# Attention with two expert layers: the gate's weight product moved behind attention, the output matrix decoded in PSUM, and edits at the start and before the experts

## The chip, the cores and the metric

The kernel runs on one core of one Trainium2 chip. The metric is the device time of one launch in microseconds. Every number of the trace comes from one profiled execution of the kernel before.

## The reference, cut to what matters

Causal attention over 4 batches of 8 heads (576 positions, head width 64) with a decay from a running sum of `s` feeds two layers. The first one multiplies by `w_in`, applies `h * clip(h + 3, 0, 6) / 6` and multiplies by `w_out`. The second one gives each of the 2304 tokens to one of 8 experts (288 tokens each), from the order of `x @ w_gate`, and runs that expert's two matrices.

```python
cum = np.cumsum(np.maximum(s, 0.0), axis=-1)
bias = -(cum[:, :, :, None] - cum[:, :, None, :])
scores = np.where(causal, -1e9, scale * (q @ k.T) + np.minimum(bias, 0.0))
attn_out = softmax(scores) @ v
...
h = x @ w_in
x2 = (h * np.clip(h + 3.0, 0.0, 6.0) / 6.0) @ w_out
...
logits = x2 @ w_gate
order = np.argsort(-logits.flatten())    # greedy, at most 288 tokens an expert
...
out[mask] = np.maximum(x2[mask] @ w1[e], 0.0) @ w2[e]
```

Logits have to be near exact, since they decide an order. So the kernel splits every f32 operand into two 16-bit parts (high and low) and sums three products.

## The kernel before, in words

**Attention** works on 16 pairs of heads. `prep` (L234) scales and splits q and k of a pair into `kq` and turns that tile with one DMA transpose on SP's queue (L253, 27 blocks of 128x128, tile `kqT`; slots 0 to 3 of it hold the first head, 4 to 7 the second, 8 the rest of both). It needs `CT`, the running sums in the layout of the positions, made once by `cumsums` (L196): PE transposes into one PSUM tile, then 18 copies on DVE (L216, L219). There is one `kq` buffer (KB=1), so the next pair is prepared only when the transpose has read it. `row_stage` finds row maxima (L298 on DVE), `col_stage` forms scores and exponentials (L364, L365 on ACT, L367 on POOL), `pv_stage` multiplies by v.

**The prologue** (`decode`, L495) reads `w_in` and then `w_out`, whose f64 words are turned into f32 by integer operations: ACT scales the high word (L511), DVE runs three operations (L512 to L514), ACT writes the f16 part (L516) and POOL the low part (L517). It does so for 32 tiles of 128x512, 16 of them for `w_out`. For `w_in` the intermediate tile lies in PSUM (tag "mm"), for `w_out` in SBUF (tag "g32", two buffers, shared with the activation of the first layer).

**The gate** (`gate_product`, L522). For eight deferred row tiles the logits are not computed from x2 but from the activation and `gm = w_out @ w_gate`, which has to be there before `logits(5)` (L580). For each of 16 slices of `w_out` two DMA transposes on SP's queue fill `wT` (one buffer), eight small matmuls on PE (L531, L532, 16 and 8 columns) go into the PSUM bank "tp", and DVE sums them into `gf` (L533).

**The first layer** (`mlp`, L634) goes through 9 units of 256 tokens: `h_step` (L548, matmuls at L556) and two `x2_tile`s (L591, L598 to L600) each. The row tiles of units 0 to 4 are done at once; for units 5 to 8 only `h_step` and `logits` run, and their eight tiles (10 to 17) are computed later, beside the routing, which is a chain of small operations on DVE and PE. Each x2 tile is stored to DRAM (`store_x2`, L624), from where the experts' tokens are gathered (L1111, POOL) and turned (L1119, SP).

**The last tile.** Expert 0's gather does not wait for tile 17: zeros are stored in its place at L853, and `tail(0)` (L1032) builds `lastsel`, a selection matrix; after the gather has been turned, four matmuls a half (L1211) pick tile 17's rows out of SBUF and DVE adds them to `xt` (L1213, two additions of 128x512).

**What sets the order.** The Python code writes the instructions in an order that `merge` (L62) makes: each stream is a generator that says how much PE time a step takes (or, by a negative number, how long it waits), and the stream with the smallest share of its budget goes next; `first=True` puts a stream ahead of the others whenever it is ready. The framework then assigns instructions to engines in the order of this program, by priority and by its own estimate of when each is ready; every engine runs its list strictly in order. In attention, each of 18 stages merges its three parts with the prologue, the gate and the first layer (15.5 us of PE time a stage). After the last stage `att_stack` is closed and the pool `late` takes its memory; then the rest of the first layer is written out alone.

```python
gts.budget = GB if t >= GT0 else 0.0
ml.budget = FILL
merge(streams + [x for x in (pro, gts, ml) if x.alive])
...
GT["keys"] = ready_keys
ml.budget = None
merge([ml])
```

Of the kernel before, what the change touches and what calls it, by code (L numbers as in the profile page):

```python
# [34 lines left out]
GB = 1200.0  # L35
# [8 lines left out]
GT0 = 2  # L44
# [57 lines left out]
def tile_attention_moe(ctx, tc, q, k, v, s, w_in, w_out, w_gate, w1, w2, out):  # L102
# [93 lines left out]
    def cumsums():  # L196
# [17 lines left out]
        for r in range(3):  # L214
            for t in range(NB):
                nc.vector.tensor_copy(CT[:, :, t:8:4, r],  # L216
                                      p[:, r, t, :].rearrange("p (n h) -> p n h", h=2))
            for h in range(2):
                nc.vector.tensor_copy(CT[h * 64:(h + 1) * 64, :, 8, r],  # L219
                                      p[h * 64:(h + 1) * 64, r, 4, h:B * H:2])  # L220
# [13 lines left out]
    def prep(n):  # L234
# [18 lines left out]
        pin(nc.sync.dma_start_transpose(out=t.rearrange("p s w x -> p (s w) x"), in_=kq.rearrange("p s w x -> p (s w x)")))  # L253
# [208 lines left out]
    def wsl(w, f):  # L462
        return w[f // 8][:, (f % 8) * 512:(f % 8 + 1) * 512]
# [31 lines left out]
    def decode(i):  # L495
        raw = RAW.pop(i)
        for f in range(2):
# [6 lines left out]
            if i < FP:  # L504
                y = psum.tile([128, 512], F32, name="mm", tag="mm", bufs=2)
            else:
                y = wts.tile([128, 512], F32, name="down", tag="g32", bufs=2)
            m = wts.tile([128, 512], F32, name="mag", tag="r", bufs=2)
            m3, y3 = (x.rearrange("p (c x) -> p c x", c=KC) for x in (m, y))
            a3 = y3.bitcast(I32) if i < FP else m3.bitcast(I32)  # L510
# [11 lines left out]
    def gate_product(fs):  # L522
        for f in fs:
            o = wts.tile([128, 2, KC, 128], F16, name="wT", bufs=1)
            o = (o[:, 0], o[:, 1].bitcast(BF))
            for t, w in zip(o, (woh, wol)):
                nc.sync.dma_start_transpose(out=t, in_=wsl(w, f))
            yield -DL[2]
            p = psum.tile([128, 16], F32, name="tp", tag="tp", bufs=TPB)
            for c in range(KC):  # L530
                nc.tensor.matmul(p, o[0][:, c, :], wgh[:, c, :], start=(c == 0), stop=False)  # L531
                nc.tensor.matmul(p[:, 0:8], o[1][:, c, :], wgh[:, c, 0:8], start=False, stop=(c == KC - 1))  # L532
            nc.vector.tensor_reduce(gf[:, f], p.rearrange("p (a e) -> p e a", a=2), axis=AX.X, op=OP.add)  # L533
            yield 8 * 27.0
# [56 lines left out]
    def x2_tile(t):  # L591
# [15 lines left out]
        if t == NT - 1:  # L607
            GT["last"] = xo
        else:
            store_x2(t, xo)  # L610
# [109 lines left out]
    gts = Stream(gates(), FT1 * 660.0)  # L720
# [30 lines left out]
    for t in range(NST):  # L751
# [16 lines left out]
    while pro.alive or gts.alive:  # L768
        raws()
        pro.budget = gts.budget = 4000.0  # L770
        merge([x for x in (pro, gts) if x.alive])
    att_stack.close()
    cpsum = ctx.enter_context(tc.tile_pool(name="cpsum", bufs=1, space=bass.MemoryType.PSUM))
    late = ctx.enter_context(tc.tile_pool(name="late", bufs=1))
    g_stack = ExitStack()
# [77 lines left out]
    store_x2(NT - 1, none)  # L853
# [37 lines left out]
    merge([ml])  # L891
# [140 lines left out]
    def tail(ph, r):  # L1032
# [19 lines left out]
        if ph == 0:  # L1052
            for j, x in ((1, RW - 128 % RW), (2, 0)):
                w = RW - x
                o = 0 if j == 1 else 128 - RW
                nc.vector.tensor_tensor(lastsel[:, o:o + w], ohr[:, NT - 1, x:],
                                        e3[:, NT - 1, j:j + 1].to_broadcast([128, w]), op=OP.mult)
# [203 lines left out]
```

## Time and profile before

| | us |
|---|---|
| median of 3 runs | 935.71 |
| lowest and highest run | 931.65, 938.3 |
| the profiled execution's own time | 931.17 |
| its span, first to last instruction | 929.4 |
| PE busy in the span | 834.4 (90%) |
| DVE, POOL, ACT busy | 568.3, 472.6, 374.9 |
| mean granted TensorE clock | 0.949 of full speed |

A share of the whole span is an average over stages: attention alone, attention with the first layer (to about 460 us), deferred units, deferred tiles with the routing (to about 684 us), and the experts. The rows below are therefore taken stage by stage. A DMA's issue is shown on SP's queue; when it lands is seen from who waits for it.

### The profile page before, as it was taken

The page shows a single profiled execution, that of the slowest core. Times are in us where ns is not written, and L with a number is a line of the kernel's source. Part 1 is how long each engine was busy: PE and PEld are TensorE (multiplying, and loading weights), DVE is VectorE, ACT ScalarE, POOL GpSimd, SP SyncE. Part 2 cuts the span into 40 slices and gives each one's busy share as a digit, 9 for nine tenths or more (in the row PEclk, how much of TensorE's full clock was granted, in tenths as well). Part 3 has the DMA queues.
Part 4 walks back from the last instruction along what each step waited for, and adds up shares of the span by engine and source line. Part 5 has one row for each costly group of instructions (what it writes and reads, how often), then busy time and mean ns, then how long its engine had stood idle before and what let it go on. Part 6 is the DMA issues. An engine that isn't in the chain of part 4 may idle for free. (4 is left out here: it accounts for less than half of the span.)

```text
span 929.4 us, 21469 instructions
## 1 busy us (share of the span) xinstructions
PE 834.4 (90%) x8553; PEld 595.1 (64%) x8553; DVE 568.3 (61%) x1705; ACT 374.9 (40%) x704; POOL 472.6 (51%) x485
## 2 busy tenths in 40 slices
PE   1688678777899999999999999999979999999996
PEld 0356457544565875866958988444447777778885
DVE  7988889875555564541356455675757877772221
ACT  2576655544344554544202222002214554455641
POOL 1466656655253564563433333003346787788951
PEclk9986778989789999999999999999989999999998
DMA  7888888789844645323220000032355765777820
GB/s 181 193 207 208 187 176 231 155 156 199 169 86 102 129 90 104 63 41 63 28 52 7 2 1 1 13 128 100 104 157 152 209 186 162 207 242 203 207 68 26
DMA packets 225524, 116.04 MB, mean 125 GB/s; under 512 B 202224, under 2 KB 202224, under 8 KB 225424
## 3 DMA queue, kind: packets, MB, share of 16 engines
q1 hardware_dynamic: 222352, 105.24, 48.1%
q0 software_dynamic: 3072, 9.44, 3.3%
q8 instruction: 67, 1.10, 0.5%
q14 instruction: 33, 0.27, 0.1%
HBM read 69.30 MB, written 9.70 MB: 85 GB/s over the span
## 5 line engine op out<-in xcount | busy, mean ns | idle before, releaser
L556 PE MATMUL mm<-xT,W 128*128 128x256 f16 (+3 forms) x2304 | 209.7, 251 | 6.1 <-DVE g L564 6.1
L1106 POOL TENSOR_TENSOR W<-stg,W 128x512 bf16<-128x512 f32 x128 | 145.0, 1159 | 100.7 <-ACT W L1104 99.8
L556 PEld LDWEIGHTS <-W 128*128 128x128 f16 (+1 forms) x2304 | 177.9, 99 | 22.9 <-DVE g L564 4.0
L1128 PEld LDWEIGHTS <-W 128*128 128x128 f16 (+1 forms) x1536 | 145.5, 98 | 42.5 <-issue 6.4
L367 POOL TENSOR_TENSOR eh<-e,eh 128x512 f16<-128x512 f32 (+1 forms) x100 | 105.5, 1070 | 99.5 <-ACT eh L365 96.6
L577 POOL TENSOR_TENSOR g<-g,g 128x512 f16<-128x512 f32 x72 | 85.5, 1187 | 125.7 <-DVE g L576 112.9
L284 PE MATMUL sc<-kqT 96*128 96x64 f16 (+10 forms) x480 | 104.7, 303 | 32.8 <-DMA kqT<-kq 18.2
L599 PE MATMUL mm<-W,g 128*128 128x512 bf16 x288 | 110.2, 383 | 3.3 <-POOL W L517 3.2
L600 PE MATMUL mm<-W,g 128*128 128x512 f16 x288 | 110.4, 384 | 0.0
L598 PE MATMUL mm<-W,g 128*128 128x512 f16 x288 | 109.6, 383 | 0.7 <-DVE g L564 0.7
L1128 PE MATMUL mm<-xt,W 128*128 128x288 f16 x768 | 105.1, 290 | 5.4 <-DVE xt L1213 4.6
L1128 PE MATMUL mm<-ht,W 128*128 128x288 f16 x768 | 102.6, 286 | 0.0
L562 ACT ACTIVATE r<-mm,three 128x512 f32<-128x512 f32 x72 | 49.4, 686 | 124.3 <-PE mm L556 116.5
L284 PEld LDWEIGHTS <-kqT 96*128 96x128 f16 (+5 forms) x768 | 54.5, 110 | 67.7 <-issue 27.2
L298 DVE TENSOR_REDUCE mx<-sc 128x1 f32<-128x384 f32 (+2 forms) x144 | 69.6, 511 | 38.0 <-PE sc L295 20.5
L364 ACT ACTIVATE e<-sc 128x512 f32<-128x512 f32 (+1 forms) x112 | 59.4, 538 | 70.0 <-PE sc L352 58.1
L564 DVE SCALAR_TENSOR_TENSOR g<-r,mm 128x512 f32<-128x512 f32 x72 | 49.3, 685 | 53.4 <-ACT r L562 52.8
L419 PE MATMUL pv<-v,eh 128*128 128x65 f16 (+1 forms) x480 | 71.4, 209 | 6.0 <-DVE x L432 6.0
L1104 ACT ACTIVATE W<-stg 128x512 f16<-128x512 f32 x128 | 75.4, 621 | 0.0
L421 PE MATMUL pv<-v,eh 128*128 128x65 f16 (+1 forms) x480 | 70.6, 205 | 1.8 <-POOL eh L367 1.8
L420 PE MATMUL pv<-v,eh 128*128 128x64 f16 (+1 forms) x480 | 71.0, 207 | 0.0
L365 ACT ACTIVATE eh<-e 128x512 f16<-128x512 f32 (+1 forms) x112 | 60.9, 570 | 13.9 <-PE pv L421 11.6
(225 smaller groups left out, 1370.3 us busy)
## 6 DMA issues: line engine op xcount, KB each, us to landing
stg<-in_moe_w_dram SPq DMA_DIRECT2D x32, 1024.0 KB
raw<-in_moe_w_in_dram SPq DMA_DIRECT2D x8, 1024.0 KB
raw<-in_moe_w_out_dram SPq DMA_DIRECT2D x8, 1024.0 KB
x2d<-xo SPq DMA_DIRECT2D x18, 256.0 KB
ldq<-in_q_dram SPq DMA_DIRECT2D x32, 128.0 KB
ldk<-in_k_dram SPq DMA_DIRECT2D x32, 128.0 KB
ldv<-in_v_dram SPq DMA_DIRECT2D x32, 128.0 KB
ldq<-in_q_dram SPq DMA_DIRECT2D x16, 32.0 KB
```

The source lines that it names most:

```text
L284: nc.tensor.matmul(o, x[0:kq], y[0:kq], start=start, stop=stop)
L367: eng.tensor_tensor(t[:, 1], e, t[:, 0], op=OP.subtract)
L419: nc.tensor.matmul(oj[:, 0:65], e[0], vv[:, 0:65], start=a, stop=False)
L420: nc.tensor.matmul(oj[:, 0:64], e[0], vv[:, 66:130], start=False, stop=False)
L556: nc.tensor.matmul(p[:, f, at:at + w], wsl(wt, ft)[:, c * 128:(c + 1) * 128], XT[b][:, c, hl, i:i + w], start=(n == 0), stop=(n == 3 * KC ...
L577: nc.gpsimd.tensor_tensor(g[:, 1].rearrange("p f x -> p (f x)"), g32, g[:, 0].rearrange("p f x -> p (f x)"), op=OP.subtract)
L598: nc.tensor.matmul(p, g[:, 0], wsl(woh, f), start=(f == 0), stop=False)
L599: nc.tensor.matmul(p, g[:, 0], wsl(wol, f), start=False, stop=False)
L600: nc.tensor.matmul(p, g[:, 1], wsl(woh, f), start=False, stop=(f == FT1 - 1))
L1104: nc.scalar.activation(h, x, AF.Copy)
L1106: nc.gpsimd.tensor_tensor(l, x, h, op=OP.subtract)
L1128: nc.tensor.matmul(p, wt[:, c, o * 128:(o + 1) * 128], x(hl, c), start=(n == 0), stop=(n == last))
```

## The change

It moves the gate's stream out of attention: its transposes go to three buffers of the pool `late`, two slices ahead of the products, and it is merged, with first right, with the rest of the first layer. It gives the decoding of `w_out` the PSUM bank "tp" (one buffer) for its intermediate tile. `cumsums` copies in four instructions. Pair 0's transpose is issued in two parts, slots 0 to 3 by SP and 4 to 8 by ACT. And the two last tiles (16 and 17) instead of one are kept out of expert 0's gather: two stores of zeros, two selection matrices, six additions instead of two. The expert outputs get three buffers of one tag.

```diff
@@ cumsums
-        for r in range(3):
-            for t in range(NB):
-                nc.vector.tensor_copy(CT[:, :, t:8:4, r],
-                                      p[:, r, t, :].rearrange("p (n h) -> p n h", h=2))
-            for h in range(2):
-                nc.vector.tensor_copy(CT[h * 64:(h + 1) * 64, :, 8, r],
-                                      p[h * 64:(h + 1) * 64, r, 4, h:B * H:2])
+        for h in range(2):
+            nc.vector.tensor_copy(CT[:, :, 4 * h:4 * h + 4, :],
+                                  p[:, :, 0:4, h:B * H:2].rearrange("p r t n -> p n t r"))
+            nc.vector.tensor_copy(CT[h * 64:(h + 1) * 64, :, 8, :],
+                                  p[h * 64:(h + 1) * 64, :, 4, h:B * H:2].rearrange("p r n -> p n r"))
@@ prep
-        pin(nc.sync.dma_start_transpose(out=t.rearrange("p s w x -> p (s w) x"), in_=kq.rearrange("p s w x -> p (s w x)")))
+        for eng, s0, s1 in ((nc.sync, 0, 9),) if n else ((nc.sync, 0, 4), (nc.scalar, 4, 9)):
+            pin(eng.dma_start_transpose(out=t[:, s0:s1].rearrange("p s w x -> p (s w) x"),
+                                        in_=kq[:, s0:s1].rearrange("p s w x -> p (s w x)")))
@@ decode
-            if i < FP:
-                y = psum.tile([128, 512], F32, name="mm", tag="mm", bufs=2)
-            else:
-                y = wts.tile([128, 512], F32, name="down", tag="g32", bufs=2)
+            y = psum.tile([128, 512], F32, name="down", tag="mm" if i < FP else "tp", bufs=2 if i < FP else TPB)
...
-            a3 = y3.bitcast(I32) if i < FP else m3.bitcast(I32)
+            a3 = y3.bitcast(I32)
@@ the gate
-    def gate_product(fs):
-        for f in fs:
-            o = wts.tile([128, 2, KC, 128], F16, name="wT", bufs=1)
...
+    def gate_turn(f):
+        o = GT["late"].tile([128, 2, KC, 128], F16, name="wT", tag="xg", bufs=3)
+        o = (o[:, 0], o[:, 1].bitcast(BF))
+        for t, w in zip(o, (woh, wol)):
+            nc.sync.dma_start_transpose(out=t, in_=wsl(w, f))
+        return o
...
     def gates():
-        for i in range(FP, 2 * FP):
-            yield from wait(lambda: ST["w"] > i)
-            yield -DL[1]
-            yield from gate_product((2 * (i - FP), 2 * (i - FP) + 1))
+        turned = []
+        for f in range(FT1 + 2):
+            if f < FT1:
+                turned.append(gate_turn(f))
+            if f >= 2:
+                gate_product(f - 2, turned[f - 2])
+                yield 8 * 27.0
+            yield -2500.0
...
-    gts = Stream(gates(), FT1 * 660.0)
+    gts = Stream(gates(), FT1 * 216.0, first=True)
...
-        gts.budget = GB if t >= GT0 else 0.0
         ml.budget = FILL
-        merge(streams + [x for x in (pro, gts, ml) if x.alive])
+        merge(streams + [x for x in (pro, ml) if x.alive])
...
-    merge([ml])
+    merge([gts, ml])
@@ the last tiles
-    store_x2(NT - 1, none)
+    for t in range(NT - 2, NT):
+        store_x2(t, none)
...
-            for j, x in ((1, RW - 128 % RW), (2, 0)):
...
+            for k, sel in enumerate(lastsel):
+                o = 0
+                for j in range(3):
+                    x = max(0, CAP - 128 * (k + 1) - j * RW)
...
-            yo = (wts, wts, ffn)[j].tile([RW, DM], F32, name="yo", tag=("wT", "x2T", "yo")[j], bufs=1)
+            yo = ffn.tile([RW, DM], F32, name="yo", bufs=3)
...
-    store_x2(NT - 1, GT["last"])
-    sp = tokens(0, sp)
+    with tc.high_priority(offset=HP):
+        sp = tokens(0, sp)
...
-    for hl in range(2):
-        p = mm_tile([128, KC, 128])
...
+    for k in (1, 0):
+        last, w = GT["last", k], 128 * (k + 1)
+        store_x2(NT - 1 - k, last)
+        with tc.high_priority(offset=HP):
+            for c0 in range(0, 2 * KC, 512 // w):
+                cs = range(c0, c0 + 512 // w)
+                p = cpsum.tile([128, len(cs), w], F32, name="pick", tag="y", bufs=YB)
...
+                x = xt[:, cs.start:cs.stop, CAP - w:]
+                nc.vector.tensor_tensor(x, x, p, op=OP.add)
```

## Rows read from the trace of the kernel before

**Rows 1.** Windows: us; PE, PEld, DVE, ACT, POOL busy (x); PEclk, DMA share, GB/s.
```profile
140.00:200.00 60.00, 48.84 (x504) 36.21 (x502) 54.67 (x90) 32.78 (x57) 39.70 (x33) 0.95 0.79 181
...
200.00:262.00 62.00, 47.05 (x443) 29.48 (x440) 31.04 (x75) 23.91 (x44) 23.49 (x23) 0.83 0.88 177
...
262.00:460.00 198.00, 197.69 (x2499) 145.73 (x2498) 94.77 (x218) 91.49 (x162) 101.72 (x93) 0.99 0.40 77
...
460.00:510.00 50.00, 48.67 (x432) 34.60 (x430) 27.58 (x134) 7.38 (x11) 18.10 (x58) 0.98 0.21 34
...
684.00:691.00 7.00, 1.81 (x12) 1.07 (x13) 2.89 (x12) 0.19 (x1) 0.59 (x1) 0.82 0.54 123
```

**Rows 2.** PE's waits from 140 to 200 us: total us, times, longest us.
```profile
PE tp L531 <- DMA wT<-W: 5.2, 4, 2.1
...
PE mm L556 <- DVE g L564: 4.1, 3, 2.2
```

**Rows 3.** PE's waits from 200 to 262 us, same columns.
```profile
PE tp L531 <- DMA wT<-W: 8.9, 4, 4.1
...
PE mm L599 <- POOL W L517: 2.2, 3, 1.0
```

**Rows 4.** Timeline of the start: start us, us, engine, line, operation, count, idle before.
```profile
10.22 0.71 DVE L216 COPY CT<-tp 128x32 f16<-128x32 f16 x4
...
12.67 0.62 DVE L219 COPY CT<-tp 64x16 f16<-64x16 f16 x2
...
13.86 4.17 SPq L253 DMA_TRANSPOSE kqT<-kq  x1
...
19.94 0.50 PE L284 MATMUL sc<-kqT 99*128 99x384 f16 x1 [11.41 <-DMA kqT<-kq]
```

**Rows 5.** Timeline of PE: first and 25th of a run of gate-sized matmuls.
```profile
503.73 0.17 PE L585 MATMUL mm<-gm,g 128*128 128x16 f16 x1
...
504.34 0.17 PE L585 MATMUL mm<-gm,g 128*128 128x16 f16 x1
```

**Rows 6.** Timeline of one pair of wT transposes, and its second product's start.
```profile
187.66 2.52 SPq L527 DMA_TRANSPOSE wT<-W  x2
...
191.41 0.18 PE L532 MATMUL tp<-wgh,wT 128*128 128x8 f16 x1
```

**Rows 7.** Groups on DVE, 135 to 242 us: count, busy us, mean ns, idle before.
```profile
L513 DVE SCALAR_TENSOR_TENSOR mag<-raw,mag 128x512 int32<-128x512 int32 x16 | 17.8, 1117 | 0.2
L514 DVE SCALAR_TENSOR_TENSOR mag<-raw,mag 128x512 int32<-128x512 int32 x16 | 13.2, 827 | 0.0
L512 DVE TENSOR_SCALAR mag<-down 128x512 int32<-128x512 int32 x16 | 8.6, 540 | 9.6 <-ACT down L511 9.6
```

**Rows 8.** Instructions of the same lines with PSUM operands: ns min/median/max, first and last start.
```profile
L512 DVE TENSOR_SCALAR mm<-mm x16: 680/690/699, 14.1 to 115.2; 128x512 int32<-128x512 int32 x16
...
L513 DVE SCALAR_TENSOR_TENSOR mm<-raw,mm x16: 678/689/708, 15.3 to 116.4; 128x512 int32<-128x512 int32 x16
...
L514 DVE SCALAR_TENSOR_TENSOR mag<-raw,mm x16: 666/678/689, 16.5 to 119.5; 128x512 int32<-128x512 int32 x16
```

**Rows 9.** Groups on DVE, 140 to 262 us: the reductions of the gate's products.
```profile
L533 DVE TENSOR_REDUCE gf<-tp 128x8 f32<-128x16 f32 x16 | 2.7, 167 | 8.2 <-PE tp L532 8.1
```

**Rows 10.** Timeline after attention: first use of the late pool, the store of zeros.
```profile
465.23 0.14 POOL L787 IOTA prio<- 128x8 f32 x1 [2.82 <-issue]
...
469.33 0.32 SPq L625 DMA_DIRECT2D x2d<-none  x1
```

**Rows 11.** Timeline before the experts: index, store of tile 16, gather, first add.
```profile
672.08 0.15 DVE L1068 SCALAR_TENSOR_TENSOR idx<-ids,ic 96x3 int32<-96x3 f32 x1
...
672.85 0.34 SPq L625 DMA_DIRECT2D x2d<-xo  x1
...
675.96 1.14 POOL L1111 DMA_INDIRECT xg<-x2d,idx  x1 [0.25 <-DVE rb L936]
...
688.90 0.69 DVE L1213 TENSOR_TENSOR xt<-xt,mm 128x512 f16<-128x512 f16 x1 [3.89 <-DMA xt<-xg]
```

More of the change, by code (lines that the diff above doesn't have):

```diff
@@ L34 @@
 WAFT = 1
-GB = 1200.0
 LG = 14
@@ L43 @@
 HE = 2
-GT0 = 2
 RD = 0
@@ L520, in tile_attention_moe, with gate_product @@
     gf = wts.tile([128, FT1, 8], F32, name="gf")
-    def gate_product(fs):
-        for f in fs:
-            o = wts.tile([128, 2, KC, 128], F16, name="wT", bufs=1)
[L525 to L534, printed above, removed]
+    def gate_turn(f):
[4 more added lines that the diff above has]
+        return o
+    def gate_product(f, o):
+        p = psum.tile([128, 16], F32, name="tp", tag="tp", bufs=TPB)
+        for c in range(KC):
+            nc.tensor.matmul(p, o[0][:, c, :], wgh[:, c, :], start=(c == 0), stop=False)
+            nc.tensor.matmul(p[:, 0:8], o[1][:, c, :], wgh[:, c, 0:8], start=False, stop=(c == KC - 1))
+        nc.vector.tensor_reduce(gf[:, f], p.rearrange("p (a e) -> p e a", a=2), axis=AX.X, op=OP.add)
     ST = {"x": 0, "w": 0, "g": 0, "rx": 0, "gx": 0}
@@ L606, in x2_tile @@
         nc.vector.tensor_tensor(xo[:, 1], p, xo[:, 0], op=OP.subtract)
-        if t == NT - 1:
-            GT["last"] = xo
+        if t >= NT - 2:
+            GT["last", NT - 1 - t] = xo
         else:
@@ L763, in tile_attention_moe @@
         pro.budget = PB[min(t, len(PB) - 1)] * 1000.0
-        gts.budget = GB if t >= GT0 else 0.0
         ml.budget = FILL
-        merge(streams + [x for x in (pro, gts, ml) if x.alive])
+        merge(streams + [x for x in (pro, ml) if x.alive])
     flush()
-    while pro.alive or gts.alive:
+    while pro.alive:
         raws()
-        pro.budget = gts.budget = 4000.0
-        merge([x for x in (pro, gts) if x.alive])
+        pro.budget = 4000.0
+        merge([pro])
     att_stack.close()
@@ L774, in tile_attention_moe @@
     late = ctx.enter_context(tc.tile_pool(name="late", bufs=1))
+    GT["late"] = late
     g_stack = ExitStack()
@@ L1052, in tail @@
         if ph == 0:
-            for j, x in ((1, RW - 128 % RW), (2, 0)):
[L1054 to L1057, printed above, removed]
+            for k, sel in enumerate(lastsel):
+                o = 0
+                for j in range(3):
+                    x = max(0, CAP - 128 * (k + 1) - j * RW)
+                    w = RW - x
+                    if w > 0:
+                        nc.vector.tensor_tensor(sel[:, o:o + w], ohr[:, NT - 1 - k, x:],
+                                                e3[:, NT - 1 - k, j:j + 1].to_broadcast([128, w]), op=OP.mult)
+                        o += w
         rhs = rt([128, NT, 2, 3], "rhs", F16)
@@ L1069, in tail @@
         IDX[ph] = idx
-    lastsel = late.tile([128, 128], F16, name="lastsel")
+    lastsel = [late.tile([128, 128 * (k + 1)], F16, name=f"lastsel{k}") for k in range(2)]
     SCAT = []
@@ L1204, in tile_attention_moe @@
     ffn = ctx.enter_context(tc.tile_pool(name="ffn", bufs=1))
-    store_x2(NT - 1, GT["last"])
-    sp = tokens(0, sp)
+    with tc.high_priority(offset=HP):
+        sp = tokens(0, sp)
     xt = XTS[0]
-    for hl in range(2):
-        p = mm_tile([128, KC, 128])
-        for c in range(KC):
-            nc.tensor.matmul(p[:, c], GT["last"][:, hl, c * 128:(c + 1) * 128], lastsel, start=True, stop=True)
-        x = xt[:, KC * hl:KC * (hl + 1), CAP - 128:]
-        nc.vector.tensor_tensor(x, x, p, op=OP.add)
+    for k in (1, 0):
[5 more added lines that the diff above has]
+                p = cpsum.tile([128, len(cs), w], F32, name="pick", tag="y", bufs=YB)
+                for c in cs:
+                    nc.tensor.matmul(p[:, c - c0], last[:, c // KC, c % KC * 128:(c % KC + 1) * 128], lastsel[k],
+                                     start=True, stop=True)
+                x = xt[:, cs.start:cs.stop, CAP - w:]
+                nc.vector.tensor_tensor(x, x, p, op=OP.add)
     for ph in range(E8):
```

## The prediction

> **What bounds the kernel now.** I read the windows first, because the share of the whole span mixes stages. From 262 to 460 us PE is busy 197.69 of 198 us, at a granted clock of 0.99: there only less work on PE helps [rows 1]. Before that it is otherwise. From 140 to 200 us PE is busy 48.84 of 60 and DVE 54.67 of 60, so DVE is nearly full. From 200 to 262 us PE is busy 47.05 of 62, DVE only 31.04, ACT and POOL less, and the granted clock is down to 0.83 of full speed [rows 1]. Nothing is full there, so somebody waits. Then I read PE's waits in these two stretches. The largest is the gate's first matmul, which waits for `wT`: 5.2 us before 200 us and 8.9 us after it, together 14.1 of the 26.1 us in which PE is idle (60 less 48.84 and 62 less 47.05) [rows 1 to 3]. Next come DVE's activation (4.1 us) and the decoded output matrix from POOL (2.2 us) [rows 2, 3]. So an order of work in which PE stands before a transposed weight slice costs more than half of PE's idle time of this stage, and `gm`, which it makes, is not used before 503.73 us, where its first reader starts [rows 5].
>
> **The start: four copies and two queues.** The 18 copies to `CT` run from 10.22 to 13.29 us (12.67 plus 0.62), 3.07 us, and the transpose of pair 0 is issued at 13.86 us, just behind them [rows 4]. The trace has no copy of the new shapes (192 and 48 elements). Below, each costs no less than one old copy's share of the row, 0.71/4 = 0.18 us, so four take 0.7; above, no more than a PSUM operation of 512 columns, 0.69 us [rows 8], so 2.8. I take 1.2, near the small ones. That gains 1.9 us, between 0.3 and 2.4. PE has nothing to do then: its first score matmul waits 11.41 us for this transpose [rows 4].
>
> The transpose takes 4.17 us to issue for 27 blocks, 0.154 us a block, and is there at 19.94 us, 1.9 us after its last issue [rows 4]. Split into 12 blocks on SP and 15 on ACT, and both at once, the longer half takes 2.3 us: a gain of 1.9 us. One behind the other, each with its landing, it is 1.85 + 1.9 + 2.3 + 1.9 = 7.95 us instead of 6.08: a loss of 1.9 us, softened by the first head's part coming earlier. No row shows transposes of two queues in flight, so I take the middle, 0. ACT's issue stands ahead of ACT's first decoding and its preparation of pair 1; pair 1 waits for this transpose anyway, since there is one `kq` buffer. The Trainium skill speaks against the two queues: "DMA: Bandwidth & Descriptors", section "Silent corruption: two transposing streams in flight at once", says that the later stream's first transpose must wait until all of the earlier stream's have completed. By that rule the halves run one behind the other, and the forecast would be 1.9 us longer; no row here shows it.
>
> **The gate leaves attention.** PE loses 128 matmuls. Their pitch shows where the same shapes run without waits: 24 steps from 503.73 to 504.34 us, 0.0254 us each [rows 5], so 3.3 us in all (their busy time is longer, since it overlaps). With the waits of 14.1 us this is 17.4 us of PE time at most. SP's queue loses 32 transposes, 16 pairs of 2.52 us [rows 6], 40 us in which the loads and the transposes of later pairs stood behind them. DVE loses 16 reductions, 2.7 us [rows 9].
>
> **The decoding in PSUM.** Per tile of 128x512 DVE's three operations take 540 + 1117 + 827 = 2484 ns in SBUF [rows 7] and 690 + 689 + 678 = 2057 ns with PSUM operands [rows 8]: 0.43 us less, 6.8 us for 16 tiles. Against it stands the one bank: ACT's scaling of the next tile has to wait until DVE's third operation on this one is done, so two tiles of a load no longer overlap. Behind that instruction on ACT stand exponentials of `col_stage`, for which POOL and then PE wait. ACT has room (busy 32.78 of 60 and 23.91 of 62 [rows 1]), but the decoding of the last loads is a chain, load after load, and I allow up to 5 us of loss for it.
>
> **What of this shortens the stage.** From 140 to 200 us DVE is the limit, so PE's waits there are worth only what DVE is relieved of: about 9 of 16 tiles and reductions, 9/16 x (6.8 + 2.7) = 5 us. From 200 to 262 us DVE has room. PE can win 8.9 us of waits and half of the matmuls, 1.7 us; what is late next is the decoded matrix (2.2 us so far) [rows 3], so I take three quarters, 8 us. With fewer gaps the granted clock of 0.83 may come back to the 0.95 of the stretch before it [rows 1]: 47.05 x (1 - 0.83/0.95) = 6 us at most, of which I take 4. Sum: a gain of 17 us. The ends are 17.4 + 6 + 2 for DVE = 25 us of gain, and 5 us of loss if nothing is won and the one bank delays the last loads.
>
> **The gate behind attention.** There PE is nearly full (48.67 of 50 us from 460 to 510 us [rows 1]), so the 3.3 us of matmuls are paid. The transposes can't start before the pool `late` has its memory, which its first user shows at 465.23 us, and perhaps only behind the zeros, stored at 469.33 us [rows 10]. A pair and the arrival of its second part took 191.41 - 187.66 = 3.75 us [rows 6], so the first product has its data between 469 and 473 us. By the program it stands some 6 us behind the end of attention's matmuls. With three buffers later slices are requested some 8 us ahead, more than these 3.75, so I see a wait at the first products only: 3 us, between 0 and 8. The stores and transposes of tiles 8 and 9 stand on SP behind at most a pair, 2.5 us, which nothing waits for soon. The chain ends at 465.23 to 469.33 plus 16 x 2.52 plus 2, 507 to 512 us, so `logits(5)`, now at 503.73, is 4 to 8 us late; unit 6's matmuls can cover that, if they stand ahead of it on PE. Cost: 6.3 us, between 3.3 and 19.
>
> **The last two tiles.** Expert 0's index is ready at 672.23 us, but the gather starts at 675.96, 3.1 us behind the store of tile 16 at 672.85 [rows 11]. That wait goes: up to 3.7 us, less the longer `lastsel`, three more small operations on the same chain, of 0.15 us like the index's own. But behind the transposes DVE now makes six additions of 0.69 us [rows 11], and the first expert matmul needs the fifth instead of the first: 4 x 0.69 = 2.8 us more. So PE's idle time before the experts (5.2 of 7 us from 684 to 691 us [rows 1]) stays about as it is: 0, between 3.1 us of gain and 2.8 of loss. The expert outputs' buffers I cost at nothing, since their number stays three; if one came late it would show as a wait of ACT for a scatter.
>
> **Sum.** -1.9 + 0 - 17 + 6.3 + 0 = -12.6 us against the profiled execution's 931.17 us, of which 929.4 is span: 918.6 us. That execution lies 4.5 us below the median of the three runs, 935.71, so the median to be expected is about 923 us.
>
> **The rivals.**
> *Everything is won.* The two queues overlap, all waits of the gate go, the clock comes back, the first products find their data: -2.4 - 1.9 - 25 + 3.3 - 3.1 = -29 us, 907. For it speaks that the waits are PE's largest; against it the full DVE before 200 us. Chance 0.15.
> *The stage keeps its length.* DVE before 200 us, and behind it the chain of loads through one bank, take the place of the gate's waits, and only 3 us are won: -1.9 - 3 + 6.3 = +1.4 us, 937. For it speaks DVE's 54.67 of 60 us; against it that DVE is half idle after 200 us. Chance 0.2.
> *The gate stalls the full engine (slower).* In attention its products cost PE 14.1 us of waits although they had a whole stage's slack in the program. If they are placed behind attention as much too early again, the same 14.1 us fall on an engine that has no gaps, with up to 8 us before `logits(5)`: 3.3 + 14.1 + 8 = 25 us, and -1.9 - 17 + 25 = +6; where the gain in attention is only half, +15. That is 942 to 951, say 946. It decides from a cost of 19 us behind attention, where it eats the gain. For it speaks that the order is estimated and not measured; against it the three buffers and an SP queue with little else. Chance 0.13.
> The forecast keeps 0.52.
>
> **How the numbers follow.** The forecast's own range is 916 to 931. The range reaches from 908, beside the first rival, to 940, which takes in the second; outside lie most of the third and some of the first. A measurement of this kernel can tell about 1% from no change, here 926.4 and 945.1 us. Faster by more: 0.15 and three quarters of the forecast, 0.54. Slower by more: most of the third rival and a tail, 0.13. Within 1%: 0.33.
>
> **What would show it.** Right, if between 140 us and the end of attention no wait for `wT` is left, the first use of the pool `late` (465.23 us [rows 10]) comes some 19 us earlier, DVE's three decoding operations take near 0.69 us each, and the first scores start 0 to 4 us earlier. Wrong in the third term, if PE's idle time in these stretches is only renamed, to DVE's activation or to the decoded matrix. Wrong in the fourth, if PE waits behind attention for `wT` by more than some 4 us, or stands before `logits(5)`. The fifth shows in PE's gap before the first expert matmul, now 5.2 us. The forecast as a whole fails if attention ends less than 8 us earlier.

## The result and the profile after

The kernel after takes 926.14 us (median of 5 runs, 923.98 to 927.23) against 935.71 in the same comparison: ratio 0.9911, interval 0.9887 to 0.9934. The forecast was 923. A second comparison on another chip gave 922.41 against 928.74, ratio 0.9934 [0.9911, 0.9957]. The kernel before measured 927 to 936 us from chip to chip, so below only ratios and positions inside a trace are compared. The profiled execution took 926.86 us with a span of 924.7, which is 4.7 less than before (before's profiled execution lies 4.5 us below its median, after's 0.7 above); where those went is read from three marks, which cut the span into three parts that add up. `late` is the first use of the pool `late` (the end of attention), the second mark is the first store of a deferred tile (the end of the stage that pays for the gate).

| | before | after | difference |
|---|---|---|---|
| start to `late` | 465.23 | 448.46 | -16.8 |
| `late` to the first deferred store | 130.4 | 144.6 | +14.3 |
| from there to the end | 333.8 | 331.6 | -2.2 |

The windows of the kernel after, core 0, with the columns of [rows 1]:

```profile
140.00:200.00 60.00, 51.31 (x505) 37.47 (x504) 52.67 (x97) 37.12 (x69) 40.90 (x36) 0.94 0.75 183
200.00:262.00 62.00, 53.04 (x528) 35.66 (x527) 39.35 (x81) 30.75 (x57) 31.67 (x32) 0.92 0.77 156
460.00:510.00 50.00, 43.29 (x494) 34.09 (x493) 21.43 (x101) 6.95 (x11) 9.24 (x8) 0.93 0.50 88
684.00:691.00 7.00, 6.29 (x54) 4.69 (x54) 6.45 (x29) 3.52 (x8) 2.90 (x4) 1.00 0.28 89
```

Against [rows 1], PE is 2.5 us busier from 140 to 200 us and 6 us busier from 200 to 262, where the granted clock is 0.92 instead of 0.83. From 460 to 510 us it has 6.7 us of idle time where there was 1.3. Now PE's waits, from 200 to 262 us and, under the dots, from 440 to 510:

```profile
PE mm L594 <- POOL W L512: 5.4, 5, 1.8
PE tp L615 <- DMA x2T<-xo: 1.4, 1, 1.4
...
PE tp L528 <- DMA wT<-W: 5.5, 6, 1.5
PE mm L580 <- DVE gm L690: 1.6, 1, 1.6
PE tp L527 <- issue: 1.2, 1, 1.2
PE tp L527 <- DMA wT<-W: 1.1, 1, 1.1
```

The waits for `wT` have left attention, and PE's idle time from 140 to 262 us falls from 26.1 to 17.7 us. That is less than the waits for `wT` had been, since a part of them only got another name: what is late next there is the decoded matrix from POOL, 5.4 us where it was 2.2 [rows 3]. The waits for `wT` stand behind attention instead. SP's queue shows why (a line is a run of issues of one kind):

```profile
448.44 3.81 SPq L521 DMA_TRANSPOSE wT<-W  x3
452.48 0.86 SPq L620 DMA_DIRECT2D x2d<-none  x2
453.39 11.70 SPq L521 DMA_TRANSPOSE wT<-W  x9
465.14 0.58 SPq L620 DMA_DIRECT2D x2d<-xo  x1
465.76 1.30 SPq L608 DMA_TRANSPOSE x2T<-xo  x1
467.17 11.30 SPq L521 DMA_TRANSPOSE wT<-W  x8
478.51 0.58 SPq L620 DMA_DIRECT2D x2d<-xo  x1
479.14 1.29 SPq L608 DMA_TRANSPOSE x2T<-xo  x1
480.54 17.85 SPq L521 DMA_TRANSPOSE wT<-W  x12
```

From 448.44 to 498.39 us the queue issues 32 transposes, 1.27 to 1.49 us apart in the mean of a run, with stores and `x2T` between. It has few pauses; its own waits in that time (446 to 500 us) are mostly for PE to free one of the three buffers, 5.2 us:

```profile
SPq L521 <- PE mm L551: 2.3, 1, 2.3
SPq L521 <- PE mm L595: 1.9, 2, 1.1
SPq L521 <- PE tp L528: 1.0, 1, 1.0
```

The work that PE has ahead of `logits(5)` was 503.73 - 465.23 = 38.5 us long before [rows 5, 10], and with the gate's matmuls 41.8. SP needs more, about 45 us even without its waits. So the first matmul of `logits(5)` starts 53.3 us behind `late`, which is 14.8 us more than before: the whole loss of the stage lies ahead of it.

```profile
501.79 0.17 PE L580 MATMUL mm<-gm,g 128*128 128x16 f16 x1 [1.61 <-DVE gm L690]
```

The decoding (groups by line, DVE, 140 to 440 us) costs what was forecast, 690 ns an operation:

```profile
L508 DVE SCALAR_TENSOR_TENSOR down<-raw,down 128x512 int32<-128x512 int32 x15 | 10.3, 689 | 0.2
L509 DVE SCALAR_TENSOR_TENSOR mag<-raw,down 128x512 int32<-128x512 int32 x15 | 10.2, 681 | 0.4
L507 DVE TENSOR_SCALAR down<-down 128x512 int32<-128x512 int32 x14 | 9.7, 692 | 3.0 <-ACT down L506 3.0
```

The start (timeline of ACT, SP and PE, with SP's wait between) and the first expert matmul (PE), to be held against [rows 4] and [rows 11]:

```profile
11.80 1.42 ACTq L250 DMA_TRANSPOSE kqT<-kq  x1
SPq L250 <- DMA kqT<-kq: 6.3, 1, 6.3
16.20 1.56 SPq L250 DMA_TRANSPOSE kqT<-kq  x1
20.04 0.50 PE L282 MATMUL sc<-kqT 99*128 99x384 f16 x1 [11.51 <-DMA kqT<-kq]
685.22 0.41 PE L1132 MATMUL mm<-xt,W 128*128 128x288 f16 x2 [0.19 <-DVE xt L1223]
```

The copies end at 11.21 instead of 13.29 us and the transpose starts 2.1 us earlier, but its second half is issued only 4.4 us behind the first, since SP's queue waits until the first half has landed (6.3 us, the line in the middle), and the first scores come at 20.04 us, as before (19.94).

### The profile page after: what moved, and what is told of

The parts are those of the page before. It is cut to its first block, busy times and chain, and to the rows that moved or that the text cites. A ratio compares the mean times of both kernels' runs of the same rounds, so it can differ in the third digit from the quotient of the medians.

```text
span 924.7 us, 21475 instructions
## 1 busy us (share of the span) xinstructions
PE 824.6 (89%) x8561; PEld 588.6 (64%) x8561; DVE 554.3 (60%) x1698; ACT 373.3 (40%) x704; POOL 467.4 (51%) x485
## 5 line engine op out<-in xcount | busy, mean ns | idle before, releaser
L551 PE MATMUL mm<-xT,W 128*128 128x256 f16 (+3 forms) x2304 | 205.3, 248 | 5.4 <-DVE g L559 3.8
L282 PE MATMUL sc<-kqT 96*128 96x64 f16 (+10 forms) x480 | 102.1, 295 | 40.3 <-DMA kqT<-kq 22.4
L1132 PE MATMUL mm<-xt,W 128*128 128x288 f16 x768 | 103.0, 286 | 2.6 <-DVE ht L1146 2.2
L282 PEld LDWEIGHTS <-kqT 101*128 101x128 f16 (+5 forms) x768 | 52.9, 107 | 72.2 <-DMA kqT<-kq 26.4
L417 PE MATMUL pv<-v,eh 128*128 128x65 f16 (+1 forms) x480 | 67.7, 203 | 1.9 <-DVE x L430 1.9
L419 PE MATMUL pv<-v,eh 128*128 128x65 f16 (+1 forms) x480 | 66.5, 199 | 2.0 <-POOL eh L365 2.0
L418 PE MATMUL pv<-v,eh 128*128 128x64 f16 (+1 forms) x480 | 66.9, 201 | 1.0 <-DVE v L220 1.0
```

Source lines behind the costliest of these rows:

```text
L282: nc.tensor.matmul(o, x[0:kq], y[0:kq], start=start, stop=stop)
L417: nc.tensor.matmul(oj[:, 0:65], e[0], vv[:, 0:65], start=a, stop=False)
L551: nc.tensor.matmul(p[:, f, at:at + w], wsl(wt, ft)[:, c * 128:(c + 1) * 128], XT[b][:, c, hl, i:i + w], start=(n == 0), stop=(n == 3 * KC ...
L1132: nc.tensor.matmul(p, wt[:, c, o * 128:(o + 1) * 128], x(hl, c), start=(n == 0), stop=(n == last))
```

## The experiments

Theory: the gate's move and the PSUM decoding win about 17 us together in attention, and the move gives back 14 us behind it, because PE's work ahead of `logits(5)` is shorter than what SP needs to turn the slices. Rivals: the gate is better left in attention, set differently; the decoding wins nothing; the loss lies in the placing of the products alone. All runs, with the ratio to the kernel before and the two marks:

| run | ratio [95%] | `late` | to the first deferred store |
|---|---|---|---|
| one_queue | 0.9932 [0.9902, 0.9962] | 448.07 | 141.6 |
| sbuf_decode | 0.9979 [0.9959, 1.0] | 454.77 | 143.5 |
| gate_as_before | 1.0132 [1.0099, 1.0166] | 481.08 | 129.1 |
| gate_late_stages | 1.0093 [1.0055, 1.0131] | 481.46 | 130.5 |
| gate_moved_only | 1.0013 [0.9995, 1.0031] | 452.49 | 143.8 |
| one_last_tile | 0.9982 [0.9965, 0.9999] | 449.00 | 142.5 |
| half_turns | 0.9874 [0.9845, 0.9903] | 446.94 | 135.8 |
| pace | 0.9812 [0.9787, 0.9836] | 447.73 | 132.4 |
| after_again | 0.9934 [0.9911, 0.9957] | 448.69 | 142.5 |
| pace_only | 0.9975 [0.9958, 0.9991] | 449.75 | 147.1 |
| logits_late | 0.9873 [0.9843, 0.9904] | 447.03 | 138.9 |
| pace_one | 0.9842 [0.9804, 0.9879] | 449.94 | 132.3 |

Before stands at 465.23 and 130.4, after at 448.46 and 144.6.

**Pair 0 on one queue** (one_queue).

```diff
-        for eng, s0, s1 in ((nc.sync, 0, 9),) if n else ((nc.sync, 0, 4), (nc.scalar, 4, 9)):
+        for eng, s0, s1 in ((nc.sync, 0, 9),):
```

> The changed kernel with pair 0's transpose issued whole by SP. In the changed kernel ACT's half is issued at 11.80 us, SP's half only at 16.20 us, and the first score matmul starts at 20.04 us, as late as before. If the two halves run one behind the other and that ate the gain of the four copies: the whole transpose is issued near 11.8 us and the first score matmul starts near 18.0 us (11.8 + 6.1). If the start counts for the end: total about 2 us shorter than the changed kernel's 926.1 us, 924. Rival: full DVE between 20 and 140 us swallows it, the first score matmul is earlier but the pool `late` is first used at 448 us as in the changed kernel, total 926.

The timeline of SP and PE in this run:

```profile
11.77 4.17 SPq L250 DMA_TRANSPOSE kqT<-kq  x1
17.89 0.50 PE L282 MATMUL sc<-kqT 99*128 99x384 f16 x1 [9.36 <-DMA kqT<-kq]
```

In one piece the transpose is there 2.15 us earlier than in two, so the second queue ate what the copies had won. But it shows neither at `late` (0.4 us) nor in the ratio, as the rival said: 2 us at the first scores are lost again before attention ends. SP issues the second pair's transpose 2.4 us earlier than in after (23.08 against 25.49 us), but the fourth pair's 5 us later (57.54 against 52.46).

**The decoding back in SBUF** (sbuf_decode).

```diff
+            if i < FP:
+                y = psum.tile([128, 512], F32, name="mm", tag="mm", bufs=2)
+            else:
+                y = wts.tile([128, 512], F32, name="down", tag="g32", bufs=2)
```

> The changed kernel with the output matrix decoded in SBUF as before (two buffers). Theory: attention became 16.8 us shorter mainly because PE no longer stands before the gate's slices; the PSUM bank is worth DVE's 0.43 us a tile, so without it the pool `late` is first used 0 to 5 us later than 448.4 us, total 926 to 931. Rival: DVE was the bound and the decoding's relief made the gain: 10 us or more later, total 936 or more. Third: the single bank costs more than it gives, since two tiles no longer overlap: earlier than 448 us, total under 925.

`late` comes 6.3 us later, a little outside the 0 to 5 us of the theory and far from the rival's 10, near the 16 x 0.43 = 6.8 us by which DVE is relieved, and the stage behind is as long as in after. PE's waits for the decoded matrix from 140 to 262 us are 11.3 us here (5.8 for ACT's part, 5.5 for POOL's), in after 7.8. The decoding in PSUM is worth some 6 us at `late`, 4 to 6 us by the ratios.

**The gate as before** (gate_as_before), inside attention, with the decoding in the same bank "tp".

```diff
-        merge(streams + [x for x in (pro, ml) if x.alive])
+        merge(streams + [x for x in (pro, gts, ml) if x.alive])
...
-    merge([gts, ml])
+    merge([ml])
```

> The changed kernel with the gate back inside attention as before (one buffer, same budgets), all else changed. Theory: the gate's move gave some 15 us in attention and took 14 us behind it. So the pool `late` is first used near 461 to 465 us, PE waits 10 us or more for `wT` between 140 and 262 us, from `late` to the first stored deferred tile it is 130 us as before (144.7 in the changed kernel), total 926 to 930. Rival: the other edits made attention's gain; then `late` stays near 450 us, the stage behind it is 130 us and the total is near 912.

This is slower than either kernel, and `late` comes 33 us later than in after, which neither theory nor rival had foreseen. ACT's waits from 140 to 440 us hold a reason:

```profile
ACT down L506 <- DVE gf L528: 16.4, 5, 5.9
```

The scaling that begins the decoding of a tile stands 16.4 us behind the gate's sums, since both take turns in one bank; in before and after this wait is not there. PE's own waits for `wT` are 6.8 us here, fewer than before's 15.4, so they are not what is new. How much of the 33 us the bank alone costs was not taken apart. With the gate inside attention `late` stands at 465.23 us with the decoding in SBUF (before) and at 481.08 in PSUM; with the gate behind it at 454.77 (sbuf_decode) and 448.46 (after). So the two edits belong together: with the gate inside attention, this PSUM bank is the wrong place for the decoding.

**The gate spread over late attention stages** (gate_late_stages), after the decoding, with one `wT`.

```diff
-        turned = []
...
+        yield from wait(lambda: ST["w"] == 2 * FP)
+        for f in range(FT1):
+            o = gate_turn(f)
+            yield -7000.0
+            gate_product(f, o)
+            yield 8 * 27.0
...
+        gts.budget = 1200.0 if t >= 11 else 0.0
```

> The changed kernel with the gate in attention's stages 11 to 16, behind the last decoding, six slices a stage at most, the product 7 us of planned time behind its transposes, one buffer. There SP's queue and the DMA engines are less than half used and PE is full. Theory: both costs of the gate are SP's pace, so spread out it costs only its matmuls, 3.3 us: `late` first used near 452 us, then 130 us to the first stored deferred tile, total about 915. Rival: PE waits for `wT` wherever the slices stand, 10 us or more in 262 to 460 us, and the total is 925 or more.

My theory fell, and the rival held. From 262 to 440 us PE is busy 159.68 of 178 us at a clock of 0.93, where after has 177.45 at 1.00, and its first waits (262 to 460 us) are

```profile
PE tp L527 <- DMA wT<-W: 14.6, 6, 4.5
PE tp L528 <- DMA wT<-W: 2.8, 6, 0.6
```

Seven microseconds of distance in the program were not enough. In some of these waits the slice stands in SP's queue behind a pair's own transpose (timeline of SP and PE):

```profile
300.66 4.40 SPq L250 DMA_TRANSPOSE kqT<-kq  x1
307.41 2.51 SPq L521 DMA_TRANSPOSE wT<-W  x2
309.88 0.19 PE L527 MATMUL tp<-wgh,wT 128*128 128x16 f16 x1 [2.65 <-DMA wT<-W]
```

In others no pair's transpose stands ahead: the product that waits until 325.03 us comes 5.7 us behind the one before, which had to free the one buffer first (its slice is issued at 320.62). The idle time (18 us), the clock (0.07 of 160 us, at most 11) and the 3.3 us of matmuls make up the 33 us by which `late` is later (in a profiled execution 5.5 us above the run's median). Since the one buffer and the shared queue come together here, this run does not show that the gate must wait wherever it stands: three buffers in the late stages were not run.

**The move alone** (gate_moved_only): the kernel before with the move and nothing else of the change but the expert outputs' buffers, one of which had the tag of `wT`.

```diff
-        merge(streams + [x for x in (pro, gts, ml) if x.alive])
+        merge(streams + [x for x in (pro, ml) if x.alive])
...
-    merge([ml])
+    merge([gts, ml])
```

> The kernel before with the gate's move alone (its transposes and products behind attention, three buffers of the pool `late`, first right), and nothing else of the change. Theory A (the move by itself is a wash, its gain inside attention is given back behind it, because SP's queue and not PE sets the pace there): the first use of the pool `late` comes some 10 us earlier than before (about 455 instead of 465.23), the stage from there to the first store of a deferred tile is 13 us longer (about 143 instead of 130.4), PE shows 8 to 12 us of waits for `wT` behind attention, and the time is that of before within 4 us. Theory B (the move carries the change's gain and the decoding in PSUM is what came for nothing): `late` comes 15 us or more earlier and the time is 7 us or more below before.

Theory A held in the sum: `late` 12.7 us earlier, the stage behind 13.5 us longer, ratio 1.0013. Its waits for `wT` behind attention came to 3.9 us, not 8 to 12; besides these there are the wait for `gm` (1.6), idle time with no releaser shown (1.1), some smaller waits, the matmuls and the clock. The move by itself wins nothing.

**One last tile** (one_last_tile): store, selection and additions as in the kernel before, and with them the order in the program, since the change also gives the turning of the tokens and the additions a higher priority.

```diff
-        if t >= NT - 2:
-            GT["last", NT - 1 - t] = xo
+        if t == NT - 1:
+            GT["last"] = xo
...
-    for t in range(NT - 2, NT):
-        store_x2(t, none)
+    store_x2(NT - 1, none)
```

> The kernel after with the last tiles as before: only tile 17 is kept out of expert 0's gather, one selection matrix, two additions. Theory A (keeping two tiles back took the gather's wait for the store of tile 16 away, and the six additions cost nothing that the end sees): PE's gap before the first expert matmul is back to some 5 us of the 7 us ahead of it, expert 0's transposes come some 3 to 4 us later against the first store of a deferred tile, and the kernel is 2 to 4 us slower than after. Theory B (my prediction's zero: the additions give back what the gather wins): within 1 us of after, with the same gap in another place.

```profile
684.60 0.40 PE L1127 MATMUL mm<-xt,W 128*128 128x288 f16 x1 [3.29 <-DVE xt L1212]
...
684.00:691.00 7.00, 6.05 (x27) 3.79 (x27) 5.09 (x17) 1.61 (x4) 4.50 (x5) 0.54 0.41 108
```

PE's wait before the first expert matmul is back (3.29 us, in after 0.19). Counted from the first deferred store, that matmul comes 93.1 us behind it, in both profiles of after 92.1. And the granted clock behind the wait is 0.54 (the window under the dots), in after 1.00, where PE's gaps are shorter (the longest 1.1 us) and stand earlier. The part behind the first deferred store is 333.0 us long, in after 331.6 and 329.6 (its two profiles): 1.4 to 3.4 us. By ratio it is 5 to 7 thousandths slower than after, some 4 to 7 us, on other chips. So the edits to the last tiles win; their size is not settled, since after's two profiles differ by 2.0 us in this part, and what the second tile wins and what the priority was not run apart.

**Half of the transposes** (half_turns); the low part of `w_out` is left out of `gm`.

```diff
-        for t, w in zip(o, (woh, wol)):
+        for t, w in zip(o[:1], (woh,)):
```

> The kernel after with only the high halves of the 16 slices turned and multiplied in the gate (the low part of the output matrix is left out of `gm`, 16 of 32 transposes and 64 of 128 matmuls are not there). Theory A (SP's queue sets the pace behind attention: 32 transposes of 1.3 to 1.5 us and the stores between them take 50 us, and the products wait for them one by one): SP has the 16 transposes issued within 25 to 30 us, PE's waits for `wT` fall from some 10 us to the first one (at most 5 us), the stage from `late` to the first deferred store is 137 us or less instead of 144.7, and the time is 6 to 10 us below after. Theory B (the place of the products in PE's order, or the clock, costs the time): the waits stay at 8 us or more, since the same products stand at the same places, and the gain is only the 1.6 us of half the matmuls.

PE's waits from 440 to 520 us:

```profile
PE mm L579 <- DVE gm L689: 2.9, 1, 2.9
PE tp L527 <- DVE beats L876: 1.3, 1, 1.3
```

With 16 transposes no wait for `wT` is left and the stage is 8.8 us shorter than in after (6.7 by after's second profile), for 1.6 us of matmuls. SP's queue is what limits it. That SP would be done within 30 us was wrong (38.6 us, since three buffers and the program's distances now hold it back), and the ratios give a gain of 3 to 6 us, not 6 to 10.

**Pace and later logits, apart and together** (pace has both edits, pace_only the first, logits_late the second).

```diff
-            yield -2500.0
+            yield -3400.0 if f != 1 else -7400.0
...
+            if u == NU - DEFER // 2:
+                continue
+            for v in (u - 1, u) if u == NU - DEFER // 2 + 1 else (u,):
+                yield from wait(lambda: ST["g"])
+                yield from logits(v)
```

> The kernel after with the gate's products set further apart behind attention (3.4 us of the program's time instead of 2.5 between slices, and 4 us more before the first product), and with the logits of unit 5 written behind unit 6's matmuls, so that they no longer stand on PE ahead of work that is ready. Theory A (the products are placed earlier than SP's queue can turn their slices): PE's waits for `wT` behind attention fall from some 10 us to 3 us or less, the stage from `late` to the first deferred store falls from 144.7 to 134 to 138 us, and the time is 6 to 10 us below after, about 917 to 920. Theory B (whatever the order, the transposes and what they take from the other queues cost the time): the waits go to other names (x2T, the activation) and the gain is under 3 us.

> The kernel after, unchanged, beside the three versions below and the kernel before on one chip, since the kernel before measured 927 to 936 us in the comparisons so far. Expected: the ratio to before of the first measurement, 0.991 within its interval, and a first deferred store some 14 us longer behind `late` than before.

> The kernel after with the gate's products set further apart (3.4 us instead of 2.5, and 4 us more before the first), but with the logits of unit 5 where they were, ahead of unit 6's matmuls. Theory A (the waits of the products for their slices cost the time): nearly all of the gain of both edits together, 0.98 to 0.985 of before; waits for `wT` gone, and at most 3 us of waiting for `gm` at unit 5's logits. Theory B (the engine loses its time before unit 5's logits, which stand ahead of unit 6's matmuls and now come later still): the wait moves to `gm`, 5 us or more, and the ratio stays at 0.988 or above.

> The kernel after with the logits of unit 5 written behind unit 6's matmuls, and the gate's pace as it was. Theory A (the products' own waits are the cost, as they stand ahead of ready matmuls): the waits for `wT` stay at 8 us or more, only the 1.6 us before unit 5's logits go, and the ratio is 0.988 to 0.991. Theory B (freeing unit 6's matmuls is what counts): waits for `wT` below 4 us and a ratio below 0.985.

Pace alone makes it worse than after, the later logits alone win 3.6 us of the stage, and both together 10.2 to 12.3 us. For both edits together theory A held; for either alone neither theory held whole. In pace_only the ratio is theory B's, but PE still waits for `wT` (11.6 us) and only 0.9 us for `gm`; in logits_late the waits for `wT` are 5.2 us and the ratio 0.9873, between the two theories. The run with pace alone shows the shortage bare (windows, then PE's timeline):

```profile
480.00:490.00 10.00, 10.00 (x118) 9.03 (x116) 7.86 (x41) 2.12 (x4) 4.24 (x4) 1.00 0.33 70
490.00:500.00 10.00, 2.05 (x37) 1.38 (x33) 1.84 (x8) 0.63 (x1) 1.53 (x2) 0.73 0.43 90
500.00:510.00 10.00, 4.95 (x99) 4.44 (x100) 2.54 (x15) 0.00 (x0) 0.00 (x0) 0.50 0.24 54
```

```profile
500.10 0.19 PE L528 MATMUL tp<-wgh,wT 128*128 128x8 f16 x1 [1.09 <-DMA wT<-W]
501.38 0.20 PE L527 MATMUL tp<-wgh,wT 128*128 128x16 f16 x1 [0.94 <-DMA wT<-W]
502.67 0.19 PE L528 MATMUL tp<-wgh,wT 128*128 128x8 f16 x1 [1.09 <-DMA wT<-W]
```

Up to 490 us PE has no gap. Then its other work ahead of `logits(5)` is used up, unit 6's matmuls stand behind in its list, and it takes the rest of the slices as SP delivers them, 1.29 us a transpose. 32 of these are 41 us, and with the stores and `x2T` between (4.6 us in after's rows) some 46, an estimate, against 41.8 us of work: by this no distance between the products can hide it. The wider distances even hold SP up, since products that come later free the three buffers later: SP waits 4.9 us for the gate's products on PE (in after 1.0) and has its last transpose issued 54.4 us behind `late` instead of 49.9. The later logits add unit 6's matmuls to the cover, but with the old distances the products still come too early (4.3 + 0.9 us of waits for `wT`). In pace both are mended:

```profile
480.00:490.00 10.00, 10.00 (x126) 9.23 (x124) 8.46 (x42) 2.30 (x4) 3.47 (x3) 1.00 0.36 74
490.00:500.00 10.00, 10.00 (x196) 10.00 (x193) 3.77 (x9) 2.72 (x4) 4.62 (x4) 1.00 0.37 68
500.00:510.00 10.00, 10.00 (x189) 10.00 (x188) 4.71 (x10) 2.09 (x4) 3.67 (x4) 1.00 0.25 56
```

The stage is 132.4 us, 2.0 more than before, and at 0.9812 of before this version beats both kernels (910.62 us against 926.96 on its chip).

> Both edits (pace and later logits) and pair 0's transpose whole on SP's queue, the version that is meant to beat both kernels. Expected 0.979 to 0.983 of before: as with both edits on the other chip (0.9812), and the start's 2 us seen in the first scores but not in the time, as in the run with one queue (0.9932 against 0.9911). If the start sets the end after all, 2 us less, 0.979.

pace_one has the same stage (132.3 us) and 0.9842, a little above the 0.979 to 0.983 expected, with an interval that overlaps with pace's. The start's 2 us are again seen in the first scores and not in the time.

## Why the prediction was right, and where it was not

The forecast (faster by 12.6 us) has the right sign, and of its size three quarters and half came, 9.6 and 6.3 us by the medians of the two comparisons. The total is nearer than its terms: in the profiled executions the span fell by 4.7 us, because attention and start won 16.8 instead of 18.9, the gate cost 14.3 instead of 6.3 and the end won 2.2 instead of 0. That the 923 us came so near the measured 926.14 owes something to luck. Its observables: no wait for `wT` up to the end of attention, `late` 16.8 us earlier where 19 were forecast, decoding at 0.69 us; only the first scores did not come earlier. The fourth term failed by the test that it named, more than 4 us of waiting behind attention and a wait before `logits(5)`.

**Attention, -17 forecast.** With the start it came to -16.8. gate_moved_only shows the move as -12.7 (on another chip), and sbuf_decode against after shows the PSUM decoding as -6.3 beside it; that these make 19.0 and not 16.8 was not settled. PE's idle time fell by 2.5 us from 140 to 200 us and by 6.0 from 200 to 262. The clock came back to 0.92, as forecast (up to 0.95). With 3.3 us of matmuls and some 5 us for the clock (53.04 us at 0.92 instead of 0.83) this makes 17, an estimate, where the forecast had added 5, 8 and 4. The price of the one bank, up to 5 us in the forecast, does not show in after, where the gate has left the bank; with the gate in place `late` comes 15.9 us later than before (gate_as_before). I had priced the bank against DVE's third operation and not against the gate's sums, which share it.

**The start, -1.9 and 0.** The copies won 2.1 us, as forecast. The queues lost them: SP's queue waits 6.3 us until ACT's half has landed, so the halves run one behind the other, at a price of 2.15 us. The rule of the Trainium skill that I weighed ("DMA: Bandwidth & Descriptors", section "Silent corruption: two transposing streams in flight at once") agrees with the trace in this. My middle of 0 was wrong there, and the term -1.9 was wrong too, since 2 us at the first scores move neither `late` nor the time. What takes them up between 20 and 140 us was not settled.

**The gate behind attention, +6.3 forecast.** This is the step that failed: +14.3. It falls into PE's idle time from 440 to 510 us, 10.2 us against 1.3; the matmuls, 3.3; and the granted clock, 0.66 and 1.00 in the two slices from 500 to 520 us against 0.88 and 0.95, at most 1.7 us: together at most 13.9. By after's second profile the stage costs 12.1. The term mis-sized is the wait, 3 us in the forecast and 8.9 us of idle time in the trace. Two sentences were wrong. "With three buffers later slices are requested some 8 us ahead, more than these 3.75, so I see a wait at the first products only" compares one slice's delay with its head start (the 3.75 us, too, only bound it from above: PE reads the second part at 191.41 us without a wait). The queue needs 1.29 us for every transpose, and slices asked for ahead only stand in it longer. And I had worked out that `logits(5)` would be 4 to 8 us late, and excused it by unit 6's matmuls "if they stand ahead of it on PE". They stood behind it, as the order of `mlp` says. I could have read that in the code instead of making it a condition. pace, pace_only and logits_late show that both halves count.

**The last two tiles, 0 forecast.** They won 1.4 to 3.4 us in the traces. The first expert matmul does wait for the fifth addition, as forecast, but the additions begin at 681.23 us instead of 688.90, since the gather starts at 660.38 and no longer 3.1 us behind the store of tile 16 [rows 11]. The gather's gain was mis-sized by a wrong reading: the index at 672.08 us is the second expert's. The instruction runs eight times, once for each expert (kernel before, times in ns, first and last start in us):

```profile
L1068 DVE SCALAR_TENSOR_TENSOR idx<-ids,ic x8: 141/148/157, 629.5 to 835.7; 96x3 int32<-96x3 f32 x8
```

Expert 0's index was there at 629.7 us, so the wait that went was not bounded by 3.7 us; in after the gather starts 4.5 us behind the store of tile 15 (655.86). About half of the 15.6 us is lost again before the additions, as SP starts to turn the tokens only at 673.65. The expert outputs' buffers cost nothing, as forecast: ACT shows no wait for a scatter. PE's gap is 0.7 of the 7 us from 684 to 691, but a part of it only moved ahead: from 676 to 691 us PE is idle for 2.5 us, before for 5.6.

**The rivals.** "The gate stalls the full engine" was the mechanism that came, at 14.3 us of cost, below the 19 from which it decides; with the move alone, without the PSUM decoding, it eats the gain (1.0013). "The stage keeps its length" fell with `late`. "Everything is won" did not come: what it lacks most is the gate's cover, and with it pace wins 16.3 us (910.62 against 926.96), of the 29 that this rival had added up.

## What to carry to other kernels

Work that is moved behind another stage needs cover as long as its slowest queue works on it (here SP's), counted in that queue's rate times its number of transfers, not in the delay of one of them. Count the matmuls that stand ahead of the first reader in the engine's own order; if they are fewer, move the reader behind more ready work first, and only then space the products. Two edits that share one PSUM bank are to be judged together: here the decoding in PSUM was worth 6 us with the gate's move, and without the move the kernel was slower than before. And a row is to be checked for the instance that it shows: an instruction that runs once for each expert has eight rows.

## What the runs showed of the hardware

A short gap on PE was followed by a lower granted clock. In pace PE waits 1.5 us for `gm` until 512.94 us, with full work up to 510 us and again behind. The windows of two microseconds:

```profile
510.00:512.00 2.00, 1.15 (x32) 1.01 (x30) 0.73 (x3) 0.69 (x1) 0.95 (x1) 1.00 0.00 0
512.00:514.00 2.00, 1.06 (x40) 1.06 (x40) 1.13 (x6) 0.00 (x0) 1.16 (x1) 0.69 0.01 4
514.00:516.00 2.00, 2.00 (x81) 2.00 (x79) 0.91 (x5) 0.00 (x0) 0.00 (x0) 0.50 0.03 8
516.00:518.00 2.00, 2.00 (x27) 1.52 (x25) 1.22 (x9) 0.00 (x0) 0.00 (x0) 0.50 0.00 0
518.00:520.00 2.00, 2.00 (x14) 1.50 (x12) 1.33 (x10) 0.00 (x0) 0.00 (x0) 0.61 0.00 0
520.00:522.00 2.00, 2.00 (x21) 1.80 (x19) 0.48 (x1) 0.69 (x1) 0.00 (x0) 1.00 0.00 0
```

Behind it the granted clock is 0.50, the level of 1.2 GHz, from 514 to 518 us, while PE is busy all the time, and back at 1.00 from 520 us. Not all matmuls pay for that. Up to 516.35 us PE runs the small ones of the logits (16 and 8 columns), which start every 0.027 us there and every 0.025 us at a clock of 1.00 [rows 5]. Only the matmuls of 256 columns behind them lose time, some 1.6 us: half of the 1.65 us up to 518 and 0.39 of the next 2 us, an estimate from the windows. So the gap of 1.5 us cost about its own length once more. In after the same stands behind the waits at 497 to 502 us (0.66 over the slice from 500 to 510), and in one_last_tile behind the wait of 3.29 us, where no small matmuls follow (0.54). In after's gaps of at most 1.1 us before the experts the clock stays at 1.00. What a gap must be like to bring the clock down was not taken apart.

The issue of a transpose has no fixed price per block: the 15 blocks on ACT's queue took 1.42 us, the 12 on SP's 1.56 and the 27 on SP's 4.17, which is 0.09, 0.13 and 0.15 us a block, so [rows 4] gave no good price for the half.
